# A different attention schedule in a relu²-attention + FFN kernel: whole-row loads, turns by transposing transfers, PSUM as four bank pairs

## The chip, the cores and the metric

The kernel runs on one core of one Trainium2 chip. The metric is device microseconds of one execution, the median of several runs. Four engines matter: TensorE (PE) multiplies into PSUM (8 banks of 512 fp32 columns in each of 128 partitions), ScalarE (ACT) and VectorE (DVE) empty PSUM, GpSimd (POOL) issues the loads that cast fp32 to bf16, and SyncE (SP) issues the transfers that need no cast. Each engine takes its instructions in program order.

## What is computed

Attention with relu² in place of softmax, over 8 batches of 12 heads, 448 tokens and 64 columns a head; its output, heads side by side, is the input of a two-layer network with a leaky relu that has one slope for each hidden column:

```python
scores = matmul(q, k.T) / sqrt(64)                    # per batch and head, 448 x 448
attn   = maximum(scores, 0) ** 2 / 448
x      = matmul(attn, v)                              # -> [3584, 768]
h      = x @ w_in                                     # 768 x 2048
g      = maximum(h, 0) + alpha * minimum(h, 0)
out    = g @ w_out                                    # 2048 x 768
```

## The kernel before

Twelve heads of a batch make three quads (four heads each); 24 quads in all. The 448 tokens are dealt as 64 x 7, so that a quad falls into seven chunks j. The program order is the order of the Python code (manual schedule); the framework adds the waits.

**Loads.** `load_batch` (L63) issues, on POOL, q and k of a batch as six transfers each (one for each quad and pair of heads; the tile's layout puts the pair's two heads side by side, so that the pieces are short), and v as one. `w_in` comes as 16 transfers, `w_out` as one. The order at the start is batch 0, `w_in`, batch 1, `w_out`; later `load_batch(b + 2)` stands at the beginning of step b. Raw tiles have two buffers a tensor.

**Turn** (`transposes`, L111). The scores need q and k with the head columns on the partitions. For each quad, PE transposes seven blocks of q and seven of k (128 x 128) into a PSUM tile of tag `mm`, and DVE copies each to SBUF (L119).

**Attention.** `scores(b, g, j)` (L121): four matmuls of 64 x 64 weights and 448 columns that lie in different quarters of the array, into a tile `sc` of two banks; relu on ACT, on DVE for j = 2 and 5 (L132, L134); a square on DVE (L136). `attnv(b, g, j)` (L139): four such matmuls that accumulate in `av` over the seven chunks of the quad; after the last one ACT scales and copies it to xT (L154). A burst is the scores of two chunks and the AV of the two chunks before them.

**FFN.** `ffn1(b, ff)` (L160): six matmuls of 448 columns for one of 16 slices of the hidden layer; ACT makes neg = relu(-h), DVE makes gT = neg * (1 - alpha) + h (L170). `ffn2(sb, c, hf)` (L175): sixteen matmuls of 384 columns for 128 of a batch pair's 896 tokens and half of the output columns; ACT copies, and after the second half SP sends two transfers of 192 KB. For an even batch c is 0 to 2, for an odd one 3 to 6.

**Order.** Batch 0's attention comes first. Then, for each batch b, the steps of its FFN1 (16) and FFN2 (6 or 8), and between them, spread evenly by an estimated cost, the bursts of batch b + 1; the turn of the next quad follows the burst that has a quad's chunk 2.

**PSUM.** `sc`: two buffers of two banks; `av`: one of two banks; `mm`: two of one bank, shared by the turn, FFN1 and FFN2.

Of the kernel before, what the change touches and what calls it, by code (L numbers as in the profile page):

```python
# [10 lines left out]
F32 = mybir.dt.float32  # L11
# [3 lines left out]

# [9 lines left out]
def kernel(  # L25
# [21 lines left out]
    raw_pool = ctx.enter_context(tc.tile_pool(name="raw", bufs=2))  # L47
    qkT_pool = ctx.enter_context(tc.tile_pool(name="qkT", bufs=2))
    at_pool = ctx.enter_context(tc.tile_pool(name="at", bufs=5))
    xT_pool = ctx.enter_context(tc.tile_pool(name="xT", bufs=2))  # L50
    g_pool = ctx.enter_context(tc.tile_pool(name="g", bufs=2))
    neg_pool = ctx.enter_context(tc.tile_pool(name="neg", bufs=3))
    o_pool = ctx.enter_context(tc.tile_pool(name="o", bufs=3))
# [6 lines left out]
    w_out_sb = singles.tile([128, KF, d_model], BF16)  # L60
    alpha_sb = singles.tile([128, KF], F32)
    beta_sb = singles.tile([128, KF], F32)


    raw = {}

    def load_batch(b, which, parts):
        src = {"q": q, "k": k, "v": v}[which]
        t = raw.get((b, which))
        if t is None:  # L70
            shape = [128, H // 2, NJ, D] if which == "v" else [128, NG, NJ, 2, D]
            t = raw_pool.tile(shape, BF16, tag=which, name=f"{which}raw")
            raw[(b, which)] = t
        if which == "v":
            flat = src[b].rearrange("(m two) (pp j) d -> (two pp) m (j d)", two=2, j=NJ)
            for lo, hi in parts:
                nc.gpsimd.dma_start(out=t[:, 2 * lo:2 * hi].rearrange("p m j d -> p m (j d)"),  # L77
                                    in_=flat[:, 2 * lo:2 * hi])
        else:
            flat = src[b].rearrange("(m two) (pp j) d -> (two pp) m j d", two=2, j=NJ)  # L80
            for lo, hi in parts:
                for g in range(lo, hi):
                    for s in range(2):
                        nc.gpsimd.dma_start(out=t[:, g, :, s], in_=flat[:, 2 * g + s])  # L84

    w_in_v = moe_w_in.rearrange("(g hf e pp) f -> hf e pp g f", hf=2, e=2, pp=64)
    w_out_v = moe_w_out.rearrange("(kf p) d -> p kf d", p=128)

    def load_w_in(lo, hi):
        for hf in range(2):  # L90
            for e in range(2):
                nc.gpsimd.dma_start(out=w_in_sb[64 * hf:64 * hf + 64, :, e, lo:hi],
                                    in_=w_in_v[hf, e, :, :, lo:hi])

    nc.sync.dma_start(out=alpha_sb, in_=moe_alpha.rearrange("(kf p) -> p kf", p=128))
    nc.vector.tensor_scalar(beta_sb, alpha_sb, -1.0, 1.0, ALU.mult, ALU.add)
    make_identity(nc, ident)
    for w in "qkv":
        load_batch(0, w, [(0, 1)])
    for w in "qkv":  # L100
        load_batch(0, w, [(1, 3)])
    for i in range(4):
        load_w_in(512 * i, 512 * i + 512)
    for w in "qkv":
        load_batch(1, w, [(0, 3)])
    nc.gpsimd.dma_start(out=w_out_sb, in_=w_out_v)


    qT, kT, att, av, xT = {}, {}, {}, {}, {}

    def transposes(b, g):  # L111
        for name, store, eng in (("q", qT, nc.vector), ("k", kT, nc.vector)):
            ps = mm_ps.tile([128, NJ, 128], BF16, tag="mm", name="tps")
            src = raw[(b, name)]
            for j in range(NJ):
                nc.tensor.transpose(ps[:, j], src[:, g, j].rearrange("p s d -> p (s d)"), ident)  # L116
            dst = qkT_pool.tile([128, 2, NJ, PP], BF16, tag=name, name=f"{name}T")
            store[(b, g)] = dst
            eng.tensor_copy(dst, ps.rearrange("p j (h c) -> p h j c", h=2))  # L119

    def scores(b, g, j):  # L121
        ps = sc_ps.tile([128, 2, 512], F32, tag="sc", name="sc")
        qt, kt = qT[(b, g)], kT[(b, g)]
        for r in range(2):
            for c in range(2):
                nc.tensor.matmul(ps[64 * c:64 * c + 64, r, :S],  # L126
                                 kt[64 * r:64 * r + 64, c, j, :],
                                 qt[64 * r:64 * r + 64, c],
                                 start=True, stop=True)
        rl = at_pool.tile([128, 2, S], BF16, tag="rl", name="rl")  # L130
        if j not in (2, 5):
# [144 lines left out]
```

## Time and profile before

| | |
|---|---|
| median of 3 runs | 524.66 us (523.15 to 525.27) |
| profiled execution, first to last instruction | 525.6 us |
| PE busy | 434.0 us, 83% |
| DVE busy | 262.0 us, 50% |
| ACT busy | 216.7 us, 41% |
| loads: packets on POOL's queue | 99,232 for 22.81 MB |

The profile is one execution. A matmul's duration is its latency, and matmuls overlap, so the pace of PE is read from the starts of instructions. In a timeline row the first number is the start, the second the time from there to the end of the group, and the bracket says how long the engine had been idle and what released it. [...] A stretch row gives the length, then busy time and count of instructions for PE, PE's weight loads, DVE, ACT and POOL, then PEclk, the mean share of the DMA engines, and GB/s.

### The profile page before, as it was taken

How to read it: one execution, taken by the hardware profiler on the slowest of the kernel's cores; microseconds unless marked ns; L12 is line 12 of the kernel's file. 1: busy time of each engine (PE TensorE's matmuls, PEld its weight loads, DVE VectorE, ACT ScalarE, POOL GpSimd, SP SyncE). 2: the span in 40 equal slices, each digit the busy share in tenths (PEclk: the TensorE clock that was granted, in tenths of full speed). 3: DMA queues.
4: the chain of work that ended last, by engine and by line, in shares of the span. 5: the costliest groups of instructions: out<-in, count | busy, mean ns of one | idle time of the engine just before them, and what ended most of it. 6: DMA issues, size and time to landing. Idle time of an engine off the chain costs nothing.

```text
span 525.6 us, 7922 instructions
## 1 busy us (share of the span) xinstructions
PE 434.0 (83%) x3344; PEld 220.5 (42%) x3344; DVE 262.0 (50%) x393; ACT 216.7 (41%) x329; POOL 112.8 (21%) x128
## 2 busy tenths in 40 slices
PE   2744979888899898898798897897888978989996
PEld 1411434443355443443345443453434533444453
DVE  1855475445653376435755365544655257633500
ACT  1443344443552363353444354534544345343411
POOL 9688066000440008000080004300000000000000
PEclk9775798998999898998999998999989999899998
DMA  9999999160492509423092325914001210012013
GB/s 93 166 187 157 205 141 113 34 110 1 30 106 58 87 0 86 53 62 52 1 104 62 77 38 38 84 46 82 2 1 30 61 31 2 0 31 61 0 43 79
DMA packets 105811, 34.34 MB, mean 65 GB/s; under 512 B 90928, under 2 KB 102192, under 8 KB 105776
## 3 DMA queue, kind: packets, MB, share of 16 engines
q0 software_dynamic: 99232, 22.81, 47.5%
q1 hardware_dynamic: 6544, 11.02, 8.5%
q8 instruction: 26, 0.43, 0.3%
q14 instruction: 9, 0.07, 0.0%
HBM read 45.62 MB, written 11.01 MB: 108 GB/s over the span
## 4 chain that ended last, share of the span: by engine, by line
PE 54%; DVE 20%; ACT 12%; POOL 5%; DMA 5%; issue 4%; ACTq 0%; POOLq 0%
PE ops L178 29%; PE hps L164 20%; DVE at L136 8%; ACT rl L132 7%; DVE rl L134 5%; DVE gT L170 5%; ACT neg L169 4%; DMA vraw<-in_v_dram 3%; PE sc L126 2%; POOL qraw L84 2%; POOL kraw L84 2%; PE av L147 2%; DVE qT L119 2%; DMA w_in_sb<-in_moe_w_in_dram 1%; ACT xT L154 1%
## 5 line engine op out<-in xcount | busy, mean ns | idle before, releaser
L164 PE MATMUL hps<-xT,w_in_sb 128*128 128x448 bf16 x768 | 175.4, 381 | 34.7 <-DVE qT L119 19.9
L178 PE MATMUL ops<-w_out_sb,gT 128*128 128x384 bf16 x896 | 151.5, 326 | 8.5 <-DVE qT L119 6.7
L136 DVE TENSOR_TENSOR at<-rl 128x896 bf16<-128x896 bf16 x168 | 102.6, 624 | 108.1 <-ACT rl L132 103.6
L170 DVE SCALAR_TENSOR_TENSOR gT<-neg,beta_sb,hps 128x448 bf16<-128x448 f32 x128 | 85.6, 678 | 95.6 <-ACT neg L169 95.6
L164 PEld LDWEIGHTS <-w_in_sb 128*128 128x128 bf16 x768 | 77.8, 104 | 127.0 <-issue 75.8
L169 ACT ACTIVATE neg<-hps 128x448 f32<-128x448 f32 x128 | 69.3, 544 | 145.1 <-PE hps L164 145.1
L132 ACT ACTIVATE rl<-sc 128x896 bf16<-128x896 f32 x120 | 106.4, 919 | 31.5 <-PE sc L126 29.7
L178 PEld LDWEIGHTS <-gT 128*128 128x128 bf16 x896 | 85.8, 98 | 72.1 <-issue 18.3
L184 ACT COPY osb<-ops 128x384 f32<-128x384 f32 x56 | 26.8, 478 | 127.0 <-PE ops L178 127.0
L84 POOL DMA_DIRECT2D qraw<-in_q_dram x48 | 46.9, 979 | 103.7 <-PE tps L116 102.7
L147 PE MATMUL av<-at,vraw 64*64 64x448 bf16 x672 | 52.0, 368 | 20.2 <-ACT xT L154 16.7
L134 DVE TENSOR_SCALAR rl<-sc 128x896 bf16<-128x896 f32 x48 | 52.1, 1085 | 14.3 <-PE sc L126 14.3
L126 PE MATMUL sc<-qT,kT 64*64 64x448 bf16 x672 | 52.6, 382 | 4.8 <-ACT rl L132 3.0
L84 POOL DMA_DIRECT2D kraw<-in_k_dram x48 | 46.8, 977 | 15.8 <-DMA w_out_sb<-in_moe_w_out_dram 13.4
L147 PEld LDWEIGHTS <-vraw 64*64 64x64 bf16 x672 | 22.4, 110 | 38.3 <-issue 23.7
L77 POOL DMA_DIRECT2D vraw<-in_v_dram x9 | 7.4, 818 | 119.4 <-PE av L147 119.4
L126 PEld LDWEIGHTS <-kT 64*64 64x64 bf16 x672 | 14.4, 108 | 35.7 <-issue 34.2
L116 PE MATMUL tps<-ident,qraw 128*128 128x128 bf16 x168 | 15.3, 239 | 12.1 <-DMA qraw<-in_q_dram 12.1
L154 ACT ACTIVATE xT<-av 128x896 bf16<-128x896 f32 x24 | 22.3, 929 | 0.0
L116 PE MATMUL tps<-ident,kraw 128*128 128x128 bf16 x168 | 15.2, 238 | 6.1 <-DMA kraw<-in_k_dram 6.1
L119 DVE COPY qT<-tps 128x896 bf16<-128x896 bf16 x24 | 14.8, 618 | 9.8 <-PE tps L116 9.8
L116 PEld LDWEIGHTS <-qraw 128*128 128x128 bf16 x168 | 10.8, 106 | 19.1 <-issue 13.2
(12 smaller groups left out, 41.0 us busy)
## 6 DMA issues: line engine op xcount, KB each, us to landing
out_dram<-osb SPq DMA_DIRECT2D x56, 192.0 KB, 2.7
qraw<-in_q_dram POOLq DMA_DIRECT2D x48, 112.0 KB, 4.1
kraw<-in_k_dram POOLq DMA_DIRECT2D x48, 112.0 KB, 4.4
vraw<-in_v_dram POOLq DMA_DIRECT2D x7, 672.0 KB, 7.4
w_in_sb<-in_moe_w_in_dram POOLq DMA_DIRECT2D x16, 192.0 KB, 7.7
w_out_sb<-in_moe_w_out_dram POOLq DMA_DIRECT2D x1, 3072.0 KB, 23.3
vraw<-in_v_dram POOLq DMA_DIRECT2D x1, 448.0 KB, 7.4
vraw<-in_v_dram POOLq DMA_DIRECT2D x1, 224.0 KB, 5.6
```

Source lines behind the costliest of these rows:

```text
L84: nc.gpsimd.dma_start(out=t[:, g, :, s], in_=flat[:, 2 * g + s])
L116: nc.tensor.transpose(ps[:, j], src[:, g, j].rearrange("p s d -> p (s d)"), ident)
L126: nc.tensor.matmul(ps[64 * c:64 * c + 64, r, :S], kt[64 * r:64 * r + 64, c, j, :], qt[64 * r:64 * r + 64, c], start=True, stop=True)
L132: nc.scalar.activation(rl, ps[:, :, :S], ACTF.Relu)
L134: nc.vector.tensor_scalar(rl, ps[:, :, :S], 0.0, None, ALU.max)
L136: nc.vector.tensor_tensor(a, rl, rl, ALU.mult)
L147: nc.tensor.matmul(ps[64 * s:64 * s + 64, r, :S], vv[64 * r:64 * r + 64, 2 * g + s, j, :], a[64 * r:64 * r + 64, s], start=(j == 0), stop= ...
L154: nc.scalar.activation(xT[b][:, g], ps[:, :, :S], ACTF.Copy, scale=out_scale)
L164: nc.tensor.matmul(ps, w_in_sb[:, km // 2, km % 2, bass.ts(ff, 128)], xT[b][:, km // 2, km % 2, :], start=(km == 0), stop=(km == KM - 1))
L169: nc.scalar.activation(neg, ps, ACTF.Relu, scale=-1.0)
L170: nc.vector.scalar_tensor_tensor(gT[b // 2][:, ff, (b % 2) * S:(b % 2) * S + S], neg, beta_sb[:, ff:ff + 1], ps, ALU.mult, ALU.add)
L178: nc.tensor.matmul(ps, gT[sb][:, ff, bass.ts(c, 128)], w_out_sb[:, ff, bass.ts(hf, 384)], start=(ff == 0), stop=(ff == KF - 1))
```

## The change

- **Loads** are made per quad, q, k and v each in one transfer of whole rows (`load_qk`, `load_v`), three raw buffers for q and k, seven for v. The order at the start is quads 0 to 2, the first half of `w_in`, then quads 3 to 5 between the other half of `w_in` and two halves of `w_out`.
- **Turns.** Quads 0 to 5 are still turned on PE (`turn_pe`), with twice as many transposes of half the width (one for each head pair), since the raw layout is no longer paired. From quad 6 on, `turn_dma`: DVE copies q and k into the paired order (`perm`), and SP issues one transposing transfer, SBUF to SBUF, of all 14 blocks into the tile `T` (four buffers).
- **PSUM** is one tile of eight banks. `take_pair` and `take_bank` hand out four bank pairs in rotation: a pair for a chunk's scores and for AV, half a pair for a transpose target, an FFN1 group or an FFN2 unit.
- **Attention** runs in bursts of two to five chunks (`run`: all scores and relus, then all squares); AV of a whole quad is one block of 28 matmuls (`attnv`). Relu is on DVE for one chunk in seven, not two.
- **Order** is written out: batch 0's quads, then FFN1 of batch 0 with quads 3 to 5 and four FFN2 units; then, for each batch b, FFN1 with two bursts of the first quad of batch b + 1 in it, and FFN2 units with five bursts between them.
- **FFN2** goes by column halves: a unit writes its own output tile (four buffers) and sends two transfers of 96 KB. gT has one buffer instead of two.

```diff
-    sc_ps = ctx.enter_context(tc.tile_pool(name="scps", bufs=2, space=bass.MemoryType.PSUM))
-    av_ps = ctx.enter_context(tc.tile_pool(name="avps", bufs=1, space=bass.MemoryType.PSUM))
-    mm_ps = ctx.enter_context(tc.tile_pool(name="mmps", bufs=2, space=bass.MemoryType.PSUM))
+    psum = ps_pool.tile([128, 8, 512], F32)
+    order = [0, 1, 2, 3]
+    spare = []
+    def take_pair():
+        p = order.pop(0)
+        order.append(p)
+        if spare and spare[0] // 2 == p:
+            spare.clear()
+        return psum[:, 2 * p:2 * p + 2]
+    def take_bank():
+        if spare:
+            return psum[:, spare.pop()]
+        p = order.pop(0)
+        order.append(p)
+        spare.append(2 * p + 1)
+        return psum[:, 2 * p]
...
+    def load_qk(n):
+        b, g = divmod(n, NG)
+        for name, src in (("q", q), ("k", k)):
+            t = raw_pool.tile([128, 2, NJ, D], BF16, tag=name, name=f"{name}raw")
             flat = src[b].rearrange("(m two) (pp j) d -> (two pp) m (j d)", two=2, j=NJ)
+            nc.gpsimd.dma_start(out=t.rearrange("p m j d -> p m (j d)"), in_=flat[:, 2 * g:2 * g + 2])
+            raw[(n, name)] = t
...
+    def turn_dma(n):
+        p = perm_pool.tile([128, 2, NJ, 2, D], BF16, tag="perm", name="perm")
+        for i, name in enumerate("qk"):
+            nc.vector.tensor_copy(p[:, i], raw.pop((n, name)).rearrange("p s j d -> p j s d"))
+        t = T_pool.tile([128, 2, NJ, 128], BF16, tag="T", name="T")
+        nc.sync.dma_start_transpose(out=t.rearrange("p a j c -> p (a j) c"),
+                                    in_=p.rearrange("p a j s d -> p (a j s d)"))
+        T[n] = t
...
+    def run(chunks):
+        got = []
+        for n, j, eng in chunks:
+            got.append((n, j, relu(score_mm(n, j), eng)))
+        for n, j, rl in got:
+            square(n, j, rl)
...
+    def prepare(n):
+        if n < NQ:
+            turn_dma(n)
+        if n + 2 < NQ:
+            load_qk(n + 2)
+            load_v(n + 2)
+    for b in range(1, B):
+        n0 = NG * (b + 1)
...
+        elif b % 2 == 0:
+            units = [(sb, c, h) for c in range(3) for h in range(2)]
+            at = {0: 0, 1: 1, 3: 2, 4: 3, 5: 4}
+        else:
+            units = [(sb, c, h) for c in range(3, 7) for h in range(2)]
+            at = {0: 0, 2: 1, 4: 2, 6: 3, 7: 4}
+        def burst(i):
...
+            if i == 0:
+                run(ch(n0, 6, 7) + ch(n0 + 1, 0, 2))
+                prepare(n0 + 2)
+            elif i == 1:
+                run(ch(n0 + 1, 2, 5))
+                attnv(n0)
+                run(ch(n0 + 1, 5, 7))
+                prepare(n0 + 3)
+            elif i == 2:
+                run(ch(n0 + 2, 0, 3))
+                attnv(n0 + 1)
+                run(ch(n0 + 2, 3, 5))
+            elif i == 3:
+                run(ch(n0 + 2, 5, 7))
+                prepare(n0 + 4)
+            else:
+                attnv(n0 + 2)
+        for ff in range(KF):
+            if not last and ff == 4:
+                run(ch(n0, 0, 3))
+            if not last and ff == 10:
+                run(ch(n0, 3, 6))
+            f1(b, ff)
+        for i, u in enumerate(units):
+            if i in at:
+                burst(at[i])
+            f2(*u)
```

Below, the three quads of batch b + 1 that step b works on (n0, n0 + 1, n0 + 2) are called A, B and C.

## Rows read from the trace of the kernel before

**Rows 1.** The page: busy time and share of each engine, and PE's granted clock

```profile
PE 434.0 (83%) x3344; PEld 220.5 (42%) x3344; DVE 262.0 (50%) x393; ACT 216.7 (41%) x329; POOL 112.8 (21%) x128
...
PEclk9775798998999898998999998999989999899998
```

**Rows 2.** Stretches of the span, and one stretch of 3.4 us

```profile
11.73:54.65 42.92, 24.76 (x241) 12.60 (x242) 25.69 (x38) 17.63 (x20) 33.52 (x41) 0.69 1.51 172
...
242.99:366.06 123.07, 105.94 (x837) 53.65 (x837) 65.17 (x99) 53.53 (x82) 25.01 (x26) 0.96 0.53 57
...
478.06:499.54 21.48, 19.64 (x101) 9.31 (x98) 10.20 (x15) 9.33 (x18) 0.00 (x0) 1.00 0.07 19
499.54:520.53 20.99, 20.96 (x128) 12.42 (x127) 0.68 (x1) 3.71 (x8) 0.00 (x0) 1.00 0.23 57
520.53:525.60 5.07, 0.00 (x0) 0.00 (x0) 0.00 (x0) 0.48 (x1) 0.00 (x0) 0.72 0.30 78
...
242.99:246.40 3.41, 3.41 (x10) 1.38 (x10) 0.88 (x2) 0.54 (x1) 0.00 (x0) 0.52 0.00 0
```

**Rows 3.** Waits from 242.99 to 366.06: total us, times, longest

```profile
PE hps L164 <- DVE qT L119: 8.1, 5, 2.2
...
PE av L147 <- ACT xT L154: 4.6, 3, 1.6
...
PE hps L164 <- DVE gT L170: 2.7, 5, 1.1
```

**Rows 4.** Timeline of PE around two turns

```profile
242.99 5.18 PE L164 MATMUL hps<-xT,w_in_sb 128*128 128x448 bf16 x18 [2.18 <-DVE qT L119]
...
279.58 0.56 PE L116 MATMUL tps<-ident,qraw 128*128 128x128 bf16 x7
...
279.99 0.55 PE L116 MATMUL tps<-ident,kraw 128*128 128x128 bf16 x7
```

**Rows 5.** Timeline of PE: FFN2, a burst, FFN2

```profile
268.84 2.76 PE L178 MATMUL ops<-w_out_sb,gT 128*128 128x384 bf16 x16 [0.24 <-DVE gT L170]
...
271.53 0.57 PE L126 MATMUL sc<-qT,kT 64*64 64x448 bf16 x8
...
271.93 0.55 PE L147 MATMUL av<-at,vraw 64*64 64x448 bf16 x8
...
272.41 2.77 PE L178 MATMUL ops<-w_out_sb,gT 128*128 128x384 bf16 x16
```

**Rows 6.** Timeline of PE: two FFN1 groups and the burst behind them

```profile
65.73 2.44 PE L164 MATMUL hps<-xT,w_in_sb 128*128 128x448 bf16 x12
68.11 0.57 PE L126 MATMUL sc<-qT,kT 64*64 64x448 bf16 x8
```

**Rows 7.** The page, groups of instructions: busy us, mean ns, idle before

```profile
L136 DVE TENSOR_TENSOR at<-rl 128x896 bf16<-128x896 bf16 x168 | 102.6, 624 | 108.1 <-ACT rl L132 103.6
...
L132 ACT ACTIVATE rl<-sc 128x896 bf16<-128x896 f32 x120 | 106.4, 919 | 31.5 <-PE sc L126 29.7
...
L84 POOL DMA_DIRECT2D qraw<-in_q_dram x48 | 46.9, 979 | 103.7 <-PE tps L116 102.7
...
L134 DVE TENSOR_SCALAR rl<-sc 128x896 bf16<-128x896 f32 x48 | 52.1, 1085 | 14.3 <-PE sc L126 14.3
...
L119 DVE COPY qT<-tps 128x896 bf16<-128x896 bf16 x24 | 14.8, 618 | 9.8 <-PE tps L116 9.8
```

**Rows 8.** Timeline of the start: v's first load, first scores, first FFN1

```profile
5.45 0.74 POOL L77 DMA_DIRECT2D vraw<-in_v_dram  x1
...
11.73 0.96 PE L126 MATMUL sc<-qT,kT 64*64 64x448 bf16 x8 [0.72 <-DVE kT L119]
...
54.65 5.48 PE L164 MATMUL hps<-xT,w_in_sb 128*128 128x448 bf16 x18
```

**Rows 9.** The page, DMA issues: count, KB each, median us to landing

```profile
out_dram<-osb SPq DMA_DIRECT2D x56, 192.0 KB, 2.7
qraw<-in_q_dram POOLq DMA_DIRECT2D x48, 112.0 KB, 4.1
...
vraw<-in_v_dram POOLq DMA_DIRECT2D x1, 224.0 KB, 5.6
```

More of the change, by code (lines that the diff above doesn't have):

```diff
@@ L38 @@
     d_model, d_ff = moe_w_in.shape
-    assert H * D == d_model and S == PP * NJ and D == 64 and H % 4 == 0
+    assert H * D == d_model and S == PP * NJ and D == 64 and H % 4 == 0 and B % 2 == 0
     NG = H // 4
@@ L104 @@
[L104 to L114, printed above, removed]
-            for j in range(NJ):
[L116 to L119, printed above, removed]
@@ L166, in ffn1, with f1_out @@
                              start=(km == 0), stop=(km == KM - 1))
+    def f1_out(ps, b, ff):
+        if b % 2 == 0 and ff == 0:
+            gT[b // 2] = g_pool.tile([128, KF, 2 * S], BF16, tag="g", name="gT")
         neg = neg_pool.tile([128, S], F32, tag="neg", name="neg")
@@ L180, in ffn2 @@
                              start=(ff == 0), stop=(ff == KF - 1))
-        if hf == 0:
-            o_sb[(sb, c)] = o_pool.tile([128, d_model], F32, tag="o", name="osb")
-        o = o_sb[(sb, c)]
-        nc.scalar.copy(o[:, bass.ts(hf, 384)], ps)
-        if hf == 1:
-            for u in range(2):
-                blk = 2 * c + u
-                b, j = 2 * sb + blk // NJ, blk % NJ
-                rows = out[b * S:(b + 1) * S].rearrange("(pp j) d -> j pp d", j=NJ)
-                nc.sync.dma_start(out=rows[j], in_=o[64 * u:64 * u + 64])
@@ L208 @@
[L208 to L245 removed]
+        o = o_pool.tile([128, HALF], F32, tag="o", name="osb")
@@ new lines, in f2, with ch @@
+        nc.scalar.copy(o, ps)
+        for u in range(2):
+            blk = 2 * c + u
+            b, j = 2 * sb + blk // NJ, blk % NJ
+            rows = out[b * S:(b + 1) * S].rearrange("(pp j) d -> j pp d", j=NJ)
+            nc.sync.dma_start(out=rows[j][:, bass.ts(hf, HALF)], in_=o[64 * u:64 * u + 64])
+    pat = "ADAAAAA"
+    def ch(n, lo, hi, p=pat):
+        return [(n, j, p[j]) for j in range(lo, hi)]
+    load_w_in(0)
+    load_w_in(1)
+    turn_pe(0)
+    run(ch(0, 0, 3))
+    load_qk(3)
@@ new lines @@
+    run(ch(0, 3, 5))
+    turn_pe(1)
+    run(ch(0, 5, 7))
+    load_v(3)
+    load_w_in(2)
+    load_w_in(3)
+    run(ch(1, 0, 2))
+    attnv(0)
+    load_qk(4)
+    load_v(4)
+    run(ch(1, 2, 4))
+    turn_pe(2)
+    run(ch(1, 4, 7))
+    load_w_out(0)
+    run(ch(2, 0, 2))
+    attnv(1)
+    load_qk(5)
+    load_v(5)
+    load_w_out(1)
+    run(ch(2, 2, 7))
+    early = []
+    for ff in range(2):
+        ps = take_bank()[:, :S]
+        f1_mm(ps, 0, ff, range(4))
+        early.append(ps)
@@ new lines @@
+    attnv(2)
+    for ff in range(2):
+        f1_mm(early[ff], 0, ff, range(4, KM))
+        f1_out(early[ff], 0, ff)
+    for ff in range(2, 6):
+        f1(0, ff)
+    turn_pe(3)
+    load_qk(6)
+    load_v(6)
+    run(ch(3, 0, 3))
+    for ff in range(6, 9):
+        f1(0, ff)
+    run(ch(3, 3, 5))
+    for ff in range(9, 11):
+        f1(0, ff)
+    run(ch(3, 5, 7))
+    for ff in range(11, 14):
+        f1(0, ff)
+    turn_pe(4)
+    load_qk(7)
+    load_v(7)
+    run(ch(4, 0, 2))
+    attnv(3)
@@ new lines @@
+    for ff in range(14, 16):
+        f1(0, ff)
+    run(ch(4, 2, 5))
+    run(ch(4, 5, 7))
+    f2(0, 0, 0)
+    turn_pe(5)
+    turn_dma(6)
+    load_qk(8)
+    load_v(8)
+    run(ch(5, 0, 2))
+    attnv(4)
+    run(ch(5, 2, 4))
+    f2(0, 1, 0)
+    run(ch(5, 4, 7))
+    turn_dma(7)
+    load_qk(9)
+    load_v(9)
+    f2(0, 2, 0)
+    attnv(5)
+    f2(0, 0, 1)
+    def prepare(n):
[4 more added lines that the diff above has]
+            load_v(n + 2)
@@ new lines @@
+    for b in range(1, B):
+        n0 = NG * (b + 1)
+        last = b == B - 1
+        sb = b // 2
+        if b == 1:
+            units = [(0, 1, 1), (0, 2, 1)] + [(0, c, h) for c in range(3, 7) for h in range(2)]
+            at = {1: 0, 3: 1, 5: 2, 7: 3, 9: 4}
+        elif b % 2 == 0:
[5 more added lines that the diff above has]
+        def burst(i):
+            if last:
+                return
+            if i == 0:
[25 more added lines that the diff above has]
+            f2(*u)
```

193 lines of the change are left out of this document (77 added, 116 removed).

## The prediction

> **What bounds the kernel now.** First the busy shares and the clock line of the page [rows 1]: TensorE (PE) is busy 83%, VectorE (DVE) 50%, ScalarE (ACT) 41%. PE is the resource to fill; the clock line shows where even a busy PE ran slowly. Then the stretches [rows 2]: two batches in the middle take 123.07 us (242.99 to 366.06; DMA moves 57 GB/s there, no bound). I compare that with what PE's instructions need when nothing holds them. An FFN2 unit of 16 matmuls is followed 2.69 us later by a burst [rows 5], 2.60 without the switch to 64-wide tiles; two FFN1 groups take 2.38 [rows 6], so about 1.14 each. The eight score matmuls of two chunks take 0.40 and the eight AV matmuls 0.48 with the switch back [rows 5]: four matmuls at once in 0.20, and 0.18 for one interruption of the FFN. Seven transposes take 0.41 [rows 4]. Two batches: 32 x 1.14 + 14 x 2.60 + 21 bursts x 0.98 + 6 turns x 0.8 = 36.5 + 36.4 + 20.6 + 4.8 = 98 us. About 25 us of 123 are lost, and the waits of that stretch name most of it [rows 3]: 8.1 us FFN1 for the turn's DVE copy (the turn holds both `mm` buffers, and its copies queue behind relu and squares), 4.6 us AV for the copy of xT (one `av` buffer), 2.7 us FFN1 for gT (two `mm` buffers). [...] Ahead of all that, FFN1 starts only at 54.65 [rows 8], and from 11.73 to there PE is busy 24.76 of 42.92 us at clock 0.69 [rows 2]. Behind it, batch 7's FFN1 takes 21.48 us, 1.34 a group, with nothing else to do.
>
> **The start.** Each quad's q and k become two transfers in whole rows instead of four of 896 short pieces. The nearest row is v of one quad, the same shape: 0.74 us to issue [rows 8], 5.6 us to land [rows 9]. k, issued second at about 1.5, lands near 7.1 (5.5 to 7.8); 14 narrower transposes at the low clock and a 0.62 us copy [rows 7] put the first scores at about 9 instead of 11.73 [rows 8]. Then three quads are paced by DVE: 1.09 (one relu) + 7 x 0.62 (squares) + 2 x 0.62 (copies) = 6.7 us each [rows 7], 20 us; AV of the third and its xT copy add 2.5. FFN1 of batch 0 runs freely from about **32**, two groups already done. Batch 1's q and k no longer stand between. Are the weights there? A quad's q, k and v are 0.69 MB in bf16, w_in and w_out 3.15 each; through w_in and quad 3, 5.9 MB are written, at 172 GB/s [rows 2] by 37 us, wanted from 43 on; w_out's halves come by 51 and 63, wanted at 62 and 77. Quad 6's q and k come at 67, when DVE asks for them: no slack, a few us if late, since relu and squares queue behind that copy.
>
> **FFN of batch 0 with quads 3 to 5** (still turned on PE): 14 x 1.14 + 4 x 2.60 + 21 x 0.20 + 3 x 1.4 + 11 interruptions x 0.18 = 16.0 + 10.4 + 4.2 + 4.2 + 2.0 = 36.8. Three turns with scores right behind: 28 transposes, 0.8 us if two 64-wide ones run together and 1.6 if not (I take 1.6; no row shows them), and 1.3 for two copies: 8.7. Low clock at first 1.7; bursts of five chunks, where four bank pairs wait for ACT's 0.92 us relu [rows 7], 2.5. Sum **50**, to 82.
>
> **The middle, batches 1 to 6.** No turn on PE, and PSUM as four pairs taken in rotation: a group's bank comes up again only after six to eight others, so the 2.7 us for gT go, and AV gets its own pair at the end of a quad, so the 4.6 us go. I laid out one even batch by hand from these durations: in FFN1 DVE falls 2 to 3 us behind after a burst of three, which is less than a bank's turn. In FFN2, AV waits about 0.1 us for an output copy, and FFN2 about 0.45 for the last relu of burst 1; I allow 0.75 a batch. Sum: 16 x 1.14 + 6 x 2.60 + 21 x 0.20 + 3 x 1.4 + 7 x 0.18 + 0.75 = 44.3; odd batches have two more units, 49.5; batch 1 has ten units, 54.7. [...] Batches 2 to 6: 3 x 44.3 + 2 x 49.5 = **231.9**. ACT gets 24 relus more (216.7 + 24 x 0.92 = 239 us) and DVE loses them (262.0 - 26, while 36 of its 48 turn copies become reorderings): both under 60% of the span.
>
> **Waits that it adds.** SP's transposing transfer waits for DVE's two reordering copies (0.62 each by the copy from PSUM, perhaps half); behind it stand the output transfers of the next FFN2 unit, and four `o` buffers cover that. DVE's copy waits for the loads issued a third of a batch earlier, and for the transfer two quads back (two `perm` buffers); gT, relu and squares stand behind it. GpSimd's loads wait for buffers of quads n-1 and n-5, long done. PE's scores wait for the transfer. That is the one that matters. For quads A and B of a batch the lead is over 20 us, for C it is short: in an even batch 11.0 us pass on PE between burst 0 and burst 2 (three units, five chunks, one AV), and DVE first works off gT, relu, three squares and two reorderings, 4.6 us: **6.4 us** are left; in an odd batch and batch 1, one unit more, 9.0.
>
> **What the transfer takes** no row shows: 448 KB in 1,792 pieces of 256 bytes, transposed. From below: an output of 192 KB on the same queue lands in 2.7 us [rows 9], the other 256 KB at 172 GB/s add 1.5: 4.2. Four of the q loads, which are in small pieces, one behind the other: 4.1 + 3 x 0.98 (the time to issue one [rows 7]) = 7.0. From above: fourteen blocks, each a transfer of 2.7 by itself: 38. The row nearest in size of piece and in bytes is the q load; I take 5.6, halfway between 4.2 and 7.0, which 6.4 hides.
>
> [...]
>
> **The end.** Batch 7: 16 x 1.14 + 8 x 2.60 = 39.0 (before 21.48 + 20.99); the tail stays at 5.07 [rows 2].
>
> **Sum.** 32 + 50 + 54.7 + 231.9 + 39.0 + 5.1 = 412.7, against a span of 525.6. The median of the runs, 524.66, is 0.9 below that span, so **412 us**.
>
> **Rivals.**
> 1. The start doesn't shrink as far (quad 6's load late, 172 GB/s not reached): 5 to 15 us more, 417 to 427. For it: the low PE share from 11.73 to 54.65 [rows 2] came with loads going all the time. Against: the short pieces, with 0.98 us to issue each [rows 7], are gone.
> 2. The transfer is late. At 12 us (about the geometric middle of 4.2 and 38) C's scores wait 5.6 us in batches 2, 4, 6 and 3.0 in 1, 3, 5: 26, and each such wait drops the clock as after the turn [rows 2, 4], 6 x 1.7 = 10: 448. [...]
> 3. Slower: the eighteen transfers follow one another on one queue and become the bound themselves. The first can start near 66, and behind quad 23's scores 57 us follow: 66 + 57 + 18 times the transfer. From **22.4 us** a transfer this is over 525.6; at 38 it is 807.
> 4. The bank rotation doesn't do what it says: PSUM is now a single tile, and if writers waited for readers of the whole tile, each FFN1 group would need its full cycle of 2.7 us (two buffers give 1.34 a group now): 128 x (2.7 - 1.14) = 200 more from FFN1 alone, over 610.
>
> **Chances.** Forecast, 400 to 420: 0.60; rival 1: 0.08; rival 2: 0.24 (0.15 up to 470, 0.09 beyond); rival 3: 0.04; rival 4: 0.02; under 398: 0.02. The range 398 to 470 holds 0.83. A measurement can tell 0.5% here. Faster: all but rivals 3 and 4 and a sliver of 2 that ends near 525: 0.93, same 0.01, slower 0.06.
>
> **What would show it.** First scores near 9 and FFN1 near 32; in the middle no wait of PE for DVE or ACT above half a us, PE's clock at 1.00, 93.8 us for two batches; FFN1 of batch 7 at 1.14 a group. A wait of PE's scores for the transfer at burst 2, with a low clock behind it, is rival 2; transfers end to end on SP's queue, rival 3; a gT wait in each group, rival 4.

## The result, and the profile after

The changed kernel takes **420.09 us** (median of 4 runs, 419.12 to 421.98) against 524.27 us for the kernel before: ratio 0.801, with a 95% interval of 0.798 to 0.804. The forecast was 412, in a range of 398 to 470. So the direction and nearly all of the gain are as forecast, and 8 us are missing.

The page of the changed kernel: its span, the busy shares (busy us, share, instructions), and the granted clock in 40 slices (PEclk, in tenths of its full value).

```profile
span 417.4 us, 7805 instructions
PE 381.9 (92%) x3176; PEld 205.6 (49%) x3176; DVE 233.1 (56%) x369; ACT 234.2 (56%) x353; POOL 64.8 (16%) x96
PEclk9999999999999999999999999999999999999999
```

Against [rows 1], PE does its work in 52 us less of busy time and is busy 92% instead of 83%; ACT has taken over relus from DVE, and both stand at 56%. The granted clock is 0.9 or more in every slice, 0.998 over the span: the slow slices of [rows 1] are gone. The first 12 us are an exception that this line doesn't show: there 14 transposes took 0.96 us where the same 14 took 0.58 later.

```profile
5.19 0.96 PE L133 MATMUL psum<-ident,qraw 128*64 128x128 bf16 x14 [5.19 <-DMA qraw<-in_q_dram]
16.34 0.58 PE L133 MATMUL psum<-ident,qraw 128*64 128x128 bf16 x14
```

The stretches of the changed kernel (columns as in [rows 2]), cut where the prediction cut them: start, FFN of batch 0, batch 1, batches 2 to 6, batch 7, tail.

```profile
0.00:29.51 29.51, 17.75 (x261) 9.72 (x262) 18.64 (x31) 18.93 (x22) 19.95 (x35) 1.00 1.13 173
29.51:75.80 46.29, 40.91 (x405) 21.32 (x404) 31.48 (x50) 27.49 (x40) 16.81 (x23) 1.00 1.27 186
75.80:133.28 57.48, 54.34 (x425) 29.86 (x424) 29.18 (x46) 30.39 (x47) 6.46 (x9) 1.00 0.68 114
133.28:373.80 240.52, 229.89 (x1867) 122.98 (x1865) 142.91 (x226) 144.41 (x219) 21.53 (x30) 1.00 0.46 85
373.80:412.80 39.00, 39.00 (x225) 21.72 (x222) 10.88 (x16) 12.52 (x24) 0.00 (x0) 1.00 0.16 40
412.80:417.40 4.60, 0.00 (x0) 0.00 (x0) 0.00 (x0) 0.48 (x1) 0.00 (x0) 0.83 0.22 55
```

| stretch | predicted | measured | difference |
|---|---|---|---|
| start, to FFN1 of batch 0 | 32 | 29.51 | -2.5 |
| FFN of batch 0 with quads 3 to 5 | 50 | 46.29 | -3.7 |
| batch 1 | 54.7 | 57.48 | +2.8 |
| batches 2 to 6 | 231.9 | 240.52 | +8.6 |
| batch 7 | 39.0 | 39.00 | 0 |
| tail | 5.07 | 4.60 | -0.5 |
| span | 412.7 | 417.40 | +4.7 |

So the miss is larger than it looks: 11.4 us in batches 1 to 6, hidden in part by 6.7 us that the beginning and the end came out shorter. The waits of the whole span (engine and line that waited, releaser: us in total, times, longest) name where it lies.

```profile
PE psum L202 <- DVE gT L211: 10.9, 8, 1.5
PE psum L154 <- DVE T L134: 7.1, 6, 1.5
PE psum L222 <- ACT rl L163: 2.9, 7, 0.4
```

The waits for the turn and for xT of [rows 3] are gone from the middle. The wait of FFN1 (L202) for gT, which the prediction had struck out, is there eight times. The timeline of batch 2 shows one of them whole (start, us to the end of the group, engine, line, operation, count, and in the bracket the idle time before it with its releaser); the two rows behind it are the same place in batch 4. The last row of batch 2 is cut off by the end of the view: that stream goes on to 24 matmuls.

```profile
133.28 4.70 PE L202 MATMUL psum<-xT,w_in_sb 128*128 128x448 bf16 x24
137.91 0.76 PE L154 MATMUL psum<-T 64*64 64x448 bf16 x12
138.61 2.44 PE L202 MATMUL psum<-xT,w_in_sb 128*128 128x448 bf16 x12
139.20 1.08 DVE L165 TENSOR_SCALAR rl<-psum 128x896 bf16<-128x896 f32 x1
140.20 1.68 DVE L170 TENSOR_TENSOR at<-rl 128x896 bf16<-128x896 bf16 x3
141.80 1.26 DVE L211 SCALAR_TENSOR_TENSOR gT<-neg,beta_sb,psum 128x448 bf16<-128x448 f32 x2
142.53 3.75 PE L202 MATMUL psum<-xT,w_in_sb 128*128 128x448 bf16 x19 [1.47 <-DVE gT L211]
...
237.84 0.76 PE L154 MATMUL psum<-T 64*64 64x448 bf16 x12
238.53 6.98 PE L202 MATMUL psum<-xT,w_in_sb 128*128 128x448 bf16 x36
```

Four groups of FFN1 (24 matmuls), a burst of three chunks (12), two groups (12), and then group 6 stands still for 1.47 us, until the first of the two gT from 141.80 has freed a bank. That gT belongs to group 4, and it had to stand behind one relu and three squares on DVE, so that it ended at about 142.4, 2.7 us behind the last matmul of its group. In batch 4 the six groups after the burst run through, 36 matmuls in one piece, with the same work on DVE. The stop comes twice in each of batches 1, 2, 3 and 5 (1.47 and 1.24 us) and never in batches 4 and 6.

The difference is in the hand-out of banks. Worked out from `take_pair` and `take_bank` (a number is a bank, s9.0 the scores of quad 9's chunk 0), the order is

```
batch 2: f1.0:3 f1.1:4 f1.2:5 f1.3:6 s9.0:0/1  s9.1:2/3  s9.2:4/5  f1.4:7 f1.5:6 f1.6:7 f1.7:0
batch 4: f1.0:2 f1.1:3 f1.2:4 f1.3:5 s15.0:6/7 s15.1:0/1 s15.2:2/3 f1.4:4 f1.5:5 f1.6:6 f1.7:7
```

In batch 2 the burst begins when half a pair, bank 7, is still left over. Three pairs go by, which brings pair 6/7 to the front of the rotation; group 4 takes the left-over half, 7, group 5 opens the pair at the front, the same one, and takes 6, and group 6 takes its other half, 7, two groups after group 4. In the whole list a group of FFN1 meets its bank again after two hand-outs in exactly eight places: groups 6 and 12 of batches 1, 2, 3 and 5. These are the eight waits.

### The profile page after: what moved, and what is told of

It reads as the page before. It is cut to its first block, busy times and chain, and to the rows that moved or that the text cites. A ratio compares the mean times of both kernels' runs of the same rounds, so it can differ in the third digit from the quotient of the medians.

```text
span 417.4 us, 7805 instructions
## 1 busy us (share of the span) xinstructions
PE 381.9 (92%) x3176; PEld 205.6 (49%) x3176; DVE 233.1 (56%) x369; ACT 234.2 (56%) x353; POOL 64.8 (16%) x96
## 4 chain that ended last, share of the span: by engine, by line
PE 76%; DVE 9%; ACT 8%; issue 3%; DMA 3%; POOL 0%; ACTq 0%; POOLq 0%
PE psum L222 35%; PE psum L202 30%; PE psum L154 6%; PE psum L180 5%; ACT rl L163 5%; DVE at L170 4%; DVE rl L165 2%; DMA T<-perm 2%; DVE gT L211 2%; DVE T L134 1%; ACT neg L210 1%; DMA kraw<-in_k_dram 1%; ACT osb L225 1%; PE psum L133 0%; ACT xT L187 0%
## 5 line engine op out<-in xcount | busy, mean ns | idle before, releaser
L202 PE MATMUL psum<-xT,w_in_sb 128*128 128x448 bf16 x768 | 150.8, 353 | 12.3 <-DVE gT L211 10.9
L222 PE MATMUL psum<-w_out_sb,gT 128*128 128x384 bf16 x896 | 151.7, 326 | 2.9 <-ACT rl L163 2.9
L211 DVE SCALAR_TENSOR_TENSOR gT<-neg,beta_sb,psum 128x448 bf16<-128x448 f32 x128 | 85.4, 678 | 89.2 <-ACT neg L210 89.2
L163 ACT ACTIVATE rl<-psum 128x896 bf16<-128x896 f32 x144 | 123.4, 928 | 14.7 <-PE psum L154 14.7
L202 PEld LDWEIGHTS <-w_in_sb 128*128 128x128 bf16 x768 | 73.8, 98 | 85.8 <-issue 19.4
L210 ACT ACTIVATE neg<-psum 128x448 f32<-128x448 f32 x128 | 69.1, 548 | 72.3 <-PE psum L202 72.3
L225 ACT COPY osb<-psum 128x384 f32<-128x384 f32 x56 | 26.8, 478 | 80.4 <-PE psum L222 80.4
L154 PE MATMUL psum<-T 64*64 64x448 bf16 x672 | 48.6, 366 | 9.7 <-DVE T L134 7.1
L91 POOL DMA_DIRECT2D qraw<-in_q_dram x24 | 17.4, 725 | 231.8 <-DVE perm L140 210.1
L180 PE MATMUL psum<-at,vraw 64*64 64x448 bf16 x672 | 37.3, 351 | 0.4 <-ACT osb L225 0.3
L180 PEld LDWEIGHTS <-vraw 64*64 64x64 bf16 x672 | 22.3, 106 | 12.4 <-issue 3.5
L91 POOL DMA_DIRECT2D kraw<-in_k_dram x24 | 17.3, 723 | 0.7 <-PE psum L154 0.4
L140 DVE COPY perm<-kraw 128x896 bf16<-128x896 bf16 x18 | 10.9, 608 | 0.0
```

What stands on the lines that cost most here:

```text
L91: nc.gpsimd.dma_start(out=t.rearrange("p m j d -> p m (j d)"), in_=flat[:, 2 * g:2 * g + 2])
L154: nc.tensor.matmul(ps[64 * c:64 * c + 64, r, :S], t[64 * r:64 * r + 64, 1, j, 64 * c:64 * c + 64], t[64 * r:64 * r + 64, 0, :, 64 * c:64 * ...
L180: nc.tensor.matmul(ps[64 * s:64 * s + 64, r, :S], vv[64 * r:64 * r + 64, s, j, :], a[64 * r:64 * r + 64, s], start=(j == 0), stop=(j == NJ ...
L202: nc.tensor.matmul(ps, w_in_sb[:, km // 2, km % 2, bass.ts(ff, 128)], xT[b][:, km // 2, km % 2, :], start=(km == 0), stop=(km == KM - 1))
L210: nc.scalar.activation(neg, ps, ACTF.Relu, scale=-1.0)
L211: nc.vector.scalar_tensor_tensor(gT[b // 2][:, ff, (b % 2) * S:(b % 2) * S + S], neg, beta_sb[:, ff:ff + 1], ps, ALU.mult, ALU.add)
```

## The experiments

Differences of spans are between single profiled executions; times and ratios are medians of several runs. Those from the second on stand on the edit of the first, save the third, and each diff is against that base (or against the kernel that the text names).

### A pair goes to the back when its second half is taken

```diff
         if spare:
-            return psum[:, spare.pop()]
+            x = spare.pop()
+            order.remove(x // 2)
+            order.append(x // 2)
+            return psum[:, x]
```

> The kernel after, with one thing changed: when the free half of a pair is used, that pair goes to the back of the rotation. Theory P (the waits of FFN1 for gT come from a pair that returns at once, because its free half was kept over a burst): the eight waits of batches 1, 2, 3 and 5, 10.9 us together, go; the span falls from 417.4 to about 406.5, batches 2, 3 and 5 to about 44.9, 49.6 and 49.6 us. Rival D (DVE's backlog of a relu and three squares holds FFN1 whichever bank it has): waits of 1.2 to 1.5 us stay behind each burst, and the span stays within 2 us of 417.

Measured: 406.12 us (405.75 to 408.48), ratio 0.775 (0.771 to 0.779), span 404.2. Batch 1 and batches 2 to 6 in its stretches, and the groups behind the first burst of batch 2:

```profile
74.87:129.63 54.76, 54.10 (x427) 29.84 (x425) 29.17 (x46) 30.56 (x47) 6.46 (x9) 1.00 0.76 124
129.63:360.50 230.87, 228.50 (x1865) 122.62 (x1864) 142.55 (x226) 144.48 (x219) 21.53 (x30) 1.00 0.48 89
134.95 6.98 PE L205 MATMUL psum<-xT,w_in_sb 128*128 128x448 bf16 x36
```

All eight waits are gone, 36 matmuls run in one piece in batch 2 as well, and the stretches are at 54.76 and 230.87, within 1.1 us of the 54.7 and 231.9 predicted. The cause of the miss in the middle is shown: not the engines, their durations or the transfers, but the lines that hand out banks. This version beats both kernels.

### All turns on PE

```diff
     def turn_dma(n):
+        return turn_pe(n)
```

> As e1, but quads 6 to 23 are turned on PE too, at the places where the transposing transfers are issued; SP issues no such transfer. Theory: each turn costs PE its 28 transposes, 0.83 us by quads 3 to 5 of the kernel after, and no wait, since the scores come 9 us or more later: 18 x 0.83 = 15 us over e1, about 421. Rival: the turn holds two banks until DVE's copies, which stand behind squares, so each turn costs 2 to 2.5 us with the clock, as in the kernel before: about 447.

Measured: 424.58 us (423.18 to 425.16), ratio 0.809 (0.804 to 0.813), span 423.0, 18.8 more than the base. A turn in batch 2:

```profile
154.67 0.76 PE L160 MATMUL psum<-T 64*64 64x448 bf16 x12
155.36 0.58 PE L136 MATMUL psum<-ident,qraw 128*64 128x128 bf16 x14
156.18 0.58 PE L136 MATMUL psum<-ident,kraw 128*64 128x128 bf16 x14 [0.24 <-ACT rl L169]
156.69 2.77 PE L228 MATMUL psum<-w_out_sb,gT 128*128 128x384 bf16 x16
```

From 155.36 to 156.69 a turn takes 1.33 us of PE, others about 0.9; 18 of them cost 18.8, 1.04 each, where 0.83 was expected. That is what the transposing transfers bring, and it is PE's own time: PE is busy 398.8 us instead of the base's 379.3. The larger part of the gain is elsewhere: even with every turn on PE the kernel is 100 us faster than before. From batch 1 on nothing waits for a turn's copy any more (8.1 us in two batches before [rows 3]); a turn itself waits 0.2 to 0.4 us for a bank in eight places.

### Fixed banks instead of the rotation

Against the changed kernel itself. Pairs 0 and 1 alternate for the scores, pair 2 serves AV, and banks 6 and 7 everything else, as in the kernel before:

```diff
-    def take_pair():
-        p = order.pop(0)
-        order.append(p)
+    def take_pair(kind):
+        if kind == "av":
+            return psum[:, 4:6]
+        p = count["sc"] % 2
+        count["sc"] += 1
...
+        x = 6 + count["mm"] % 2
+        count["mm"] += 1
+        return psum[:, x]
```

> The kernel after, with PSUM divided as in the kernel before: two pairs for scores, one for AV, two single banks for turns, FFN1 and FFN2. Theory (the rotation carries much of the gain): FFN1 groups at 1.34 instead of 1.14 us, 128 x 0.2 = 25; waits for gT behind two bursts in each FFN1, about 2 us each, 27; the third chunk of each burst waits for a relu, about 4 us a batch, 24: about 490. Rival (order and turns carry the gain, banks little): below 435.

Measured: 464.09 us (463.04 to 465.13), ratio 0.885 (0.878 to 0.891), span 463.4. Its two largest waits of this kind, and a stretch of FFN1 in batch 2:

```profile
PE psum L150 <- ACT rl L159: 36.2, 45, 1.2
PE psum L198 <- DVE gT L207: 10.6, 42, 1.0
149.00 2.43 PE L198 MATMUL psum<-xT,w_in_sb 128*128 128x448 bf16 x12
151.65 2.43 PE L198 MATMUL psum<-xT,w_in_sb 128*128 128x448 bf16 x12 [0.21 <-DVE gT L207]
154.01 0.57 PE L150 MATMUL psum<-T 64*64 64x448 bf16 x8
155.52 0.38 PE L150 MATMUL psum<-T 64*64 64x448 bf16 x4 [0.94 <-ACT rl L159]
```

In this program order the rotation is worth 46 us, and 59 with the first experiment's edit. The size was forecast too high (about 490): gT waits of 2 us behind the bursts didn't come, the longest is 1.0. The likely reason, not tested by itself, is that the third chunk of a burst already waits 0.94 us for ACT's relu, so that DVE can catch up. A wait also costs more than its idle time: two groups take 2.65 us with a wait of 0.21, against 2.31 in a stream (24 matmuls in 4.63 us in the base), so 0.13 comes on top. In these rows the matmuls ahead of the wait end at 151.43 and those behind it start at 151.65, with no overlap; in the stream they overlap: 24 start within 4.63 us, where one takes 0.35.

### The third quad's transfer one burst later

`prepare(n0 + 2)` moves from burst 0 into burst 1, ahead of `prepare(n0 + 3)`.

> As e1, but the transposing transfer of each batch's third quad is issued one burst later, just ahead of the next one. It lands 6.9 us after its issue in the kernel after; DVE's copies end about 4 us behind burst 1 and the scores want it 5.3 us behind burst 1. Theory (price of a late transfer as in the prediction): a wait of about 5.7 us in each of batches 1 to 6, 34 us, and 1.7 us each for the lower clock behind it, 10: about 451. Without a drop of the clock about 441. If the transfer is hidden anyway: 407.

Measured: 448.90 us, ratio 0.856 (0.849 to 0.862), span 447.3. The wait in batch 2, its sum, and the stretch behind it:

```profile
174.50 1.33 PE L157 MATMUL psum<-T 64*64 64x448 bf16 x12 [5.86 <-DMA T<-perm]
175.62 2.83 PE L183 MATMUL psum<-at,vraw 64*64 64x448 bf16 x28
PE psum L157 <- DMA T<-perm: 32.0, 7, 6.1
174.50:178.50 4.00, 4.00 (x44) 2.01 (x48) 2.69 (x4) 1.73 (x2) 0.00 (x0) 0.50 1.25 192
```

The transfer was issued at 167.4, landed 7.0 us later, and released the scores at 174.50. Behind the wait the granted clock is 0.50, and 28 AV matmuls take 2.83 us instead of the 1.49 to 1.58 that they take where no such wait stands before them. Of the 43 us over the base 32 are waits; the 11 that are left fit the clock, about 2 us behind each of the longer waits. So the transfer's place matters as the second rival said, and the changed kernel has it just early enough.

### The turns on PE ahead of their use

In the FFN of batch 0 each turn moves ahead of work that hides DVE's copies of T:

```diff
-    for ff in range(2, 6):
+    for ff in range(2, 4):
         f1(0, ff)
     turn_pe(3)
+    for ff in range(4, 6):
+        f1(0, ff)
...
+    turn_pe(4)
     for ff in range(11, 14):
         f1(0, ff)
-    turn_pe(4)
...
-    f2(0, 0, 0)
     turn_pe(5)
+    f2(0, 0, 0)
```

> As e1, with the turns of quads 3, 4 and 5 on PE issued two or three FFN1 groups, or one FFN2 unit, ahead of their scores instead of right before them. Theory: the scores' waits for the two copies (1.51, 1.51 and 0.86 us in e1) go, 3.9 us: span 404.2 to about 400.3. Rival: the copies now stand ahead of gT on DVE and the wait moves to FFN1: 403 to 404.

Measured: 405.22 us (403.94 to 406.95), ratio 0.772 (0.769 to 0.774), span 403.5. The waits for T went from 7.5 to 4.1 us, and batch 0's FFN ended at 71.81 instead of 74.87, but the span gained only 0.7:

```profile
77.48 0.76 PE L157 MATMUL psum<-T 64*64 64x448 bf16 x12 [0.97 <-DMA T<-perm]
254.19 0.76 PE L157 MATMUL psum<-T 64*64 64x448 bf16 x12 [1.55 <-DMA T<-perm]
```

The gain came, and went into waits for transposing transfers: 2.9 us in three places. The first is quad 6's, which PE now asks for 3 us sooner; the others are in the middle, which the edit doesn't touch. There the transfer itself took longer: the scores at 254.19 waited for the one issued at 245.89, which landed 8.3 us later, where the base's takes 6.8 in that place. (The longest, 11.4 us from 251.44, held up nothing.) What sets its time was the question of the last two experiments.

### Short pieces again, for q and k only

```diff
-            t = raw_pool.tile([128, 2, NJ, D], BF16, tag=name, name=f"{name}raw")
+            t = raw_pool.tile([128, 2, NJ, D + 16], BF16, tag=name, name=f"{name}raw")
...
+            for s in range(2):
+                nc.gpsimd.dma_start(out=t[:, s, :, :D], in_=flat[:, 2 * g + s])
```

> As e1, but q and k of a quad are loaded as in the kernel before, by four transfers of 896 short pieces (the raw tile's rows are padded so that the pieces stay apart). Theory (whole rows pay at the start only): k of quad 0 lands about 3 us later, first scores near 11.5 instead of 8.7, FFN1 of batch 0 from 33 to 36 instead of 30, nothing in the middle: span 407 to 411. Rival (the loads' short pieces were the main cost of the old start): FFN1 from 40 or later, 415 or more.

Measured: 412.33 us, ratio 0.785 (0.782 to 0.788), span 411.1, 6.9 more than the base. First scores at 9.87 instead of 8.69, FFN1 free at 31.16 instead of 29.96: the start itself lost only 1.2. The rest is one place:

```profile
66.63 0.62 DVE L144 COPY perm<-qraw 128x896 bf16<-128x896 bf16 x1 [2.97 <-DMA qraw<-in_q_dram]
68.85 0.62 DVE L144 COPY perm<-kraw 128x896 bf16<-128x896 bf16 x1 [1.60 <-DMA kraw<-in_k_dram]
70.52 4.44 PE L226 MATMUL psum<-w_out_sb,gT 128*128 128x384 bf16 x16 [4.54 <-DVE rl L169]
```

Quad 6's q and k come late, DVE's copies wait for them, the relu stands behind the copies, and FFN2 waits 4.54 us for the relu's bank, with the low clock behind it (granted 0.69 from 70.5 to 76.0; 16 matmuls in 4.44 us, elsewhere 2.77). It is the chain that the prediction named for quad 6 ("no slack"). Whole rows bring 7 us here, and only because they come on time.

### One chunk at a time in FFN1

```diff
-            if not last and ff == 4:
-                run(ch(n0, 0, 3))
-            if not last and ff == 10:
-                run(ch(n0, 3, 6))
+            if not last and ff in (2, 4, 6, 8, 10, 12):
+                run(ch(n0, ff // 2 - 1, ff // 2))
```

> As e1, but the six chunks in each FFN1 come one at a time, after every second group, not as two bursts of three. Theory: four more interruptions a batch at 0.1 to 0.18 us each, six batches, 2.4 to 4.3 us: span 406.6 to 408.5. Rival (short bursts leave DVE less backlog and so less waiting): at or below 404.

Measured: 415.54 us (413.75 to 417.92), ratio 0.791 (0.788 to 0.795), span 414.8, 10.6 more.

```profile
79.47 0.38 PE L157 MATMUL psum<-T 64*64 64x448 bf16 x4 [2.64 <-DMA T<-perm]
136.84 2.44 PE L205 MATMUL psum<-xT,w_in_sb 128*128 128x448 bf16 x12
139.22 0.38 PE L157 MATMUL psum<-T 64*64 64x448 bf16 x4
```

FFN1 of batch 2 takes 20.78 us with six stops and 19.84 with two in the base: 0.94 for four stops more, 0.24 each, and 5.6 in six batches, above the 2.4 to 4.3 that was expected. The other 5 us are transfers again: quad 6's scores now come two groups sooner and wait 2.64 us, with 1.6 more behind (12 matmuls in 4.06 us instead of 2.44; the mean granted clock of this execution was 0.996), and one of batch 4 waits 1.65. Long bursts are worth 5.6 us, then, and the rest hangs on the transfer.

### Two relus of a quad on DVE instead of one

`pat` becomes "AADAADA", two chunks of seven on DVE.

> As e1, but two relus in seven are on DVE, as in the kernel before, not one. ACT gets 24 x 0.92 = 22 us less work and DVE 24 x 1.09 = 26 us more. Theory (neither engine sets the pace): within 2 us of 404.2. Rival: DVE's longer backlog behind each burst makes FFN1 wait for gT, 1 us each at twelve places: about 416; or the 0.43 us waits of FFN2 for ACT's relu go, about 401.

Measured: 408.77 us (407.70 to 412.00), ratio 0.780 (0.776 to 0.784), span 406.4, 2.2 more. FFN2's waits for ACT's relu (0.43 us in each batch) went, scores wait 0.3 us for DVE's in three batches instead, the start is 1.0 longer (FFN1 free at 30.97), and one wait for a transfer came up in batch 4:

```profile
257.39 0.76 PE L157 MATMUL psum<-T 64*64 64x448 bf16 x12 [2.27 <-DMA T<-perm]
```

The middle is near a balance of the two engines: which of them takes a relu is worth no more than the 2 us of the start and of one late transfer, and the intervals of this kernel and the base overlap.

### Loads moved in the program

Against the kernel with early turns: `prepare` only turns, and the loads stand in FFN1 ahead of groups 2 and 8 and behind burst 1.

> The kernel of e6_early_turns with one thing more: the loads of a quad's q, k and v no longer follow the turn of another quad at once; two of a batch's three stand in its FFN1 (before groups 2 and 8), one behind the second burst. So no load runs beside the transposing transfer for which PE's scores wait soonest. Theory L (the transfer's time is set by the load beside it: in e6 it landed 6.8 to 11.4 us after its issue with a load behind it, 3.5 to 3.9 for the last three, which have none): the transfers issued in the first burst of a batch land in 3.5 to 4.5 us, the waits of scores for a transfer go from 2.9 us in all to under 0.5, and the span from 403.5 to 400.6 (400 to 401.5). Rival (the last three land sooner for another reason, such as the outputs queued behind them): those transfers still land in 6.8 to 11 us, the waits stay at 2 to 3 us and the span at 403 to 404. A second rival: the loads now in FFN1 come late for DVE's reordering copies, whose wait holds up squares and gT: 1 to 3 us more than e6, and rows of DVE waiting for q or k.

Measured: 403.66 us (402.95 to 404.12), ratio 0.773 (0.766 to 0.779), span 401.6. The span is near what was expected, but not for the reason: **the loads did not move**. The rows of the first burst of batch 2, POOL's load and SP's transfer:

```profile
151.14 0.72 POOL L94 DMA_DIRECT2D qraw<-in_q_dram  x1 [28.66 <-DVE perm L143]
151.43 1.48 SPq L145 DMA_TRANSPOSE T<-perm  x1
DMA to landing us min/median/max: 7.0/7.0/7.0
```

POOL has waited 28.66 us for DVE's copy: it is ahead of the other engines, and a load of q goes out as soon as the copy frees its buffer, 0.29 us ahead of the transfer that the same copies feed. The place in the program decides nothing here. The transfer still takes 7.0 us, and this run shows nothing on the theory; its smaller waits (0.8 us for transfers) lie within what the transfers scatter.

### Loads held back by v's buffers

Against the kernel with early turns: v gets five buffers instead of seven and is loaded ahead of q and k, so that a quad's load waits for an AV.

```diff
-    v_pool = ctx.enter_context(tc.tile_pool(name="v", bufs=7))
+    v_pool = ctx.enter_context(tc.tile_pool(name="v", bufs=5))
...
-            load_qk(n + 2)
             load_v(n + 2)
+            load_qk(n + 2)
```

> In e10 no load moved: POOL runs ahead of the others, and a load of q leaves as soon as DVE's copy has freed one of the three raw buffers, wherever it stands in the program; its first row of a batch, at 151.14, lies 0.26 us before the transfer's issue as it did in e6. Here the kernel of e6_early_turns gets a real dependence instead: v has five buffers, not seven, and stands ahead of q and k in the queue, so that a quad's load waits for the AV five quads before it, which comes at the end of a quad's scores. In the first burst of a batch, where the copy frees a buffer, no load can then leave before the AV of the second burst, 4 us later. Theory L (the transfer's time is set by the load that runs beside it): the transfers of the first burst land in 3.5 to 4.5 us instead of 6.9 to 8.3, no scores wait for a transfer in the middle batches, and the span is 400.5 to 401.5. Rival (they land sooner at the end of the program for another reason): those transfers still take 6.8 us or more, and the span is 401.5 to 404. A second rival: the loads, now later, hold up DVE's copies and the gT behind them: over 404.

Measured: 405.12 us (404.05 to 405.76), ratio 0.772 (0.767 to 0.777), span 403.5. The same place of batch 2, and the landings of all 18 transfers (shortest, median, longest); the last line is that of the changed kernel:

```profile
154.12 1.47 SPq L145 DMA_TRANSPOSE T<-perm  x1
154.89 0.72 POOL L101 DMA_DIRECT2D vraw<-in_v_dram  x1 [25.77 <-PE psum L157]
DMA to landing us min/median/max: 3.4/4.4/18.9
DMA to landing us min/median/max: 3.5/6.9/14.4
```

The load leaves 0.77 us behind the transfer's issue instead of 0.29 ahead of it (not 4 us behind: that AV ends sooner than expected), and that is enough: the transfers of the first bursts of batches 1 to 5 land in 4.4, 5.1, 4.0, 4.7 and 3.4 us, the median of all falls from 6.9 to 4.4, and no scores of the middle wait for one. The theory holds there. The time didn't follow: quad 6's transfer, among the last loads of the start, took 17.7 us and its scores waited 2.09, and the start came out 1.5 us longer (FFN1 free at 31.14 instead of 29.64). No row ties that part to the loads: PE kept the slow pace of the start to about 17 us instead of 12, and the first 28 AV matmuls took 2.61 us instead of 1.49. This variant, the two before it on early turns and the first experiment can't be told apart by their intervals: they all end at 404 to 406 us.

## Why the prediction was right and where it failed

**Right: what bounds the kernel.** PE as the resource to fill, and the three waits of [rows 3] as what keeps it idle, gave the sum. (Of the 25 us lost in those two batches the three are 15.4. A mean clock of 0.96 over 123 us [rows 2] is about 5 more, an estimate, and 3.5 are waits of the same kinds, 2.2 of FFN2 for the turn and 1.3 of FFN1 for xT.) Without the bank mistake the middle is 285.6 us long (54.76 + 230.87) against 286.6 predicted: the prices per unit taken from the lines of before (1.14 a group, 2.60 a unit, 0.20 a chunk, 0.18 an interruption) hold in the new order as a sum, though not each by itself: an interruption by a single chunk measured 0.24. The sums of the middle hold no term for a low clock, and no row of before shows that none is needed; in the changed kernel the granted clock there was 1.00.

**How much each step brings is known only in part.** Taken back one at a time, the transfers cost 18.8 us, the bank rotation 59, whole rows 6.9, long bursts 5.6. That is 90 of the 121 us between the kernel before and the base, and such single costs need not add up. The written-out order and AV by whole quads were never taken back alone, so their share isn't shown.

**Failed: "a group's bank comes up again only after six to eight others".** One even batch was laid out by hand. What came out of it fits a batch in which no half pair is left over when a burst begins: batches 4 and 6 are such batches, and they ran in 44.2 us each where 44.3 was predicted (3 and 5 in 52.3 where 49.5 was); in batches 1, 2, 3 and 5 the step is false, groups 6 and 12 come back after two, and the 2.7 us of gT waits that the prediction struck out came back as 10.9. The "2 to 3 us" that DVE falls behind a burst was right, and with a reuse after two groups, 2.3 us, it decides. The rest of the 12.4 us between this kernel and the base in batches 1 to 6 is the overlap lost around eight waits (0.13 each, the figure from the fixed banks, so an estimate) and about half a us.

**Start: 32 predicted, 29.51.** First scores came at 8.24 (about 9 predicted; the transposes ran at the slow pace that was assumed). The three quads took the 20 us predicted, but not by DVE's pace alone: from 8.24 to 28.49 DVE was busy 17.1 us and ACT 16.7, and PE waited for both in turn, so the agreement is partly luck. The copy of the third quad's xT added 1.0, where AV and copy were put at 2.5, as most of AV ran while the last squares were made.

**FFN of batch 0: 50 predicted, 46.29.** 28 half-width transposes take 0.83 us (34.89 to 35.31 to the end of the second half), the lower of the two values, and the three turns 6.8 with their waits, not 8.7; the 1.7 of low clock, half of the 3.4 us at 0.52 of [rows 2], didn't come (1.00 in that stretch); the other waits of the stretch sum to 1.5, where 2.5 was put down for the bursts of five.

**The transfer: 5.6 estimated, 6.9 measured, inside the bounds of 4.2 and 7.0; right with nothing to spare.** In batch 4 of the changed kernel it was issued at 258.14, landed 6.8 us later, and the scores began at 264.98, behind a weight load that had waited 0.5 us for it; the lead, predicted at 6.4, was about that long. What the estimate had no term for is the load beside it: alone the same transfer takes 3.5 us, under the lower bound. So the estimate came near by luck, as the middle between two rows of other transfers. The step behind it is that GpSimd's loads were to wait for buffers "long done". In the trace they wait for the very copies that feed the transfer, and leave together with it (in batch 4 the load of q at 257.85, the transfer at 258.14):

```profile
POOL qraw L91 <- DVE perm L140: 210.1, 14, 31.7
```

The prediction's bound from above, 38 us for fourteen blocks each a transfer by itself, was far off: in the changed kernel the 18 transfers of fourteen blocks landed 3.5 to 14.4 us after their issue. The first two, among the loads of the start, took 14.4 and 13.6; the last three, issued behind the last load, 3.8, 3.5 and 3.5; the 13 others 6.7 to 10.1, nine of them 6.7 to 7.2. That is 3.5 us for 448 KB transposed and alone, against 2.7 for a plain transfer of 192 KB in [rows 9].

**Rivals.** The first (a longer start) didn't come, but the experiment with short pieces shows its chain, within 6.9 us in all. The second didn't come; the late transfer shows its price: waits of about 5.8 us and 2 of clock behind each, where the rival had 5.6 or 3.0 and 1.7. (That it ends at 448.9 and the rival had 448 is chance: 43 us on a base of 406 against 36 on 412.) The third needed 22.4 us a transfer; the longest of any was 18.9. The fourth didn't come: in the stream of 24 matmuls in 4.70 us each group starts without waiting for the one before.

**Batch 7 and the tail.** 39.0 predicted and measured; 4.6 instead of 5.07, with last transfers of 96 KB instead of 192.

**From the span to the time.** The prediction took the time as 0.9 below the span, by the profiled span and the median of other executions. Within one execution the time is 1.7 to 1.9 above the span in every kernel here (419.12 and 417.4 in the changed one). That is 2.6 us of the 8.

## What to carry to other kernels

When buffers come from a rotation that serves two sizes, write out the hand-out for every phase in which it can start, and look for the shortest distance of reuse rather than for a typical one: one state of the rotation cost 11 us of waits here, and an edit of four lines in the hand-out bought them back. A gain ahead of a transfer with no slack was handed on to that transfer (3.1 us gained by the early turns, 0.7 left in the span), so look at what is late next before you count it. And a load that was moved in the program left where it had left before, when its buffer came free, since its issuing engine had run ahead and waited 28.66 us for that; a change of what it waits for moved it, by 1.06 us in batch 2.

## What the runs showed of the hardware

- A transposing transfer of 448 KB within SBUF, fourteen 128x128 blocks, landed in the changed kernel 3.5 to 3.8 us after its issue where no load left any more (three transfers), 6.7 to 7.2 in nine places and 8.0 to 10.1 in four where a quad's load of whole rows left 0.3 us ahead of it, and 13.6 and 14.4 among the loads of the start. That the load's head start decides was tried (the first bursts' transfers: 6.9 to 8.3 us with it, 3.4 to 5.1 with the load 0.8 to 3.3 us behind in batches 2 to 5); what the longest ones share was not. SP's queue took 1.47 to 2.48 us to issue one in the middle, and 7.27 at 72.52, while the one before it landed only at 78.3; in the first experiment 8.61.
- A stop of a stream of 128-wide matmuls for four 64x64 ones cost 0.24 us more than the same four in a longer burst (FFN1 of batch 2: 20.78 us with six stops, 19.84 with two), and a wait of 0.21 us in a stream of FFN1 groups cost about 0.13 us more than its idle time (two groups in 2.65 us against 2.31).
- The granted clock stayed at 1.00 in the stretches with the 1.47 us waits, and stood at 0.50 for 4 us behind the wait of 5.86 us; in the kernel before it was 0.52 behind one of 2.18 [rows 2, 4]. The length of one wait doesn't tell: with two relus on DVE there was a wait of 2.27 us (257.39), and the mean granted clock of that execution was 1.000; in the kernel before it was 0.50 from 300.9 to 304.3, behind waits of 1.51 and 0.77 us with only 14 transposes and four short matmuls between them.
- The granted clock reads 1.00 over the first 29.5 us of the changed kernel, and still 14 transposes took 0.96 to 0.99 us up to 12 us and 0.56 to 0.58 from 16 us on.
